# Where the second pair's sums of weight blocks are made in a fused attention and gated-MLP kernel

## The chip, the cores and the metric

The kernel runs on one core of a Trainium2 chip. A core has five engines that run side by side, each through its own instruction stream in order: TensorE (PE, the matmuls, whose weight loads are shown apart as PEld), VectorE (DVE), ScalarE (ACT), GpSimd (POOL) and SyncE (SP, which here only issues DMAs). DMAs are issued from the streams of SP and ACT: a DMA whose buffer isn't free yet, or whose data isn't made yet, holds what stands behind it in the same stream. Sixteen DMA engines carry all transfers. Matmul results land in PSUM, which has eight banks here of 128 x 512 fp32.

The metric is the time of one execution on the device in microseconds (us); lower is better. The kernel before takes 739.52 us, the median of three runs from 738.2 to 742.48.

## The reference

Two branches read the same layer-normed input `xn` (2048 rows, 512 columns, fp32), and their product is added to `x`.

```
xn = layernorm(x)
# branch A: 32 heads of 16; each row attends to 8 rows: itself and those 2, 4, .. 14 back
q, k, v = split(xn @ wqkv)
s = windowed_attention(q, k, v) @ wo

# branch B: gMLP with F = 1792, Fh = 896
z  = gelu(xn @ w_in)                       # first projection: z1, second: the gate's
z1 = z[:, :896];  z2 = layernorm(z[:, 896:])
g  = w_sp @ z2 + b_sp                      # the mixing over the 2048 rows
b  = (z1 * g) @ w_out

out = x + s * silu(b)
```

## The kernel before

**Precision.** Every fp32 operand of a large matmul is split into a high part (rounded by ScalarE, `AF.Copy` to fp32r, L191) and a low part (the rest, by VectorE, L192). A product is three matmuls: high by high, high by low, low by high. `prep` (L171) fetches a raw 128 x 512 weight block by an SP DMA (`fetch`, L166), and splits it into one of eight weight pairs.

**Order of the stages on TensorE.** First q, k and v (`pair`, L379 to L381, stored to DRAM), then z1 (L649: seven blocks `f` of 128 columns, four row chunks `c` each, gelu, stored to DRAM by ACT as `z_d`), then the gate's second projection, called z2 (L735: an index `i` over eight pairs of row tiles `i` and `8 + i`), then the mixing (matmuls at L771), then `b` (L1000 to L1002) and last `s`, which needs attention's output.

**Attention** runs beside all this on VectorE, with GpSimd for one fold: `scores` (L523), `heads` (L530), `weighted` (L567), and a transpose (L590) whose result SP stores as `o_d` (L593). It is traced with the lowest priority (except `heads`), so it fills VectorE where nothing else is ready.

**The mixing.** The transposed `w_sp` is a grid of four column chunks `c` of 512 output rows and 16 blocks of 128 input rows. A pair `a` is the two chunks 2a and 2a + 1. With the input rows halved (blocks 0 to 7 and 8 to 15), each pair is a 2 x 2 block matrix, which is multiplied with z2 (halved by rows, and by columns into three blocks on either side of an odd one) in seven block products instead of eight. Each product is called m1 to m7 with the pair's letter, and runs over eight blocks `s` (`block_product`, L794); with the odd column it has 12 matmuls for each block. m1 and m2 use weight blocks as they are in the input. The products m3 to m7 use sums of weight blocks, and z2 operands that are combined in the z2 stage (`combine`, L709, stored as `t_d`). Order: m1a, m1b, m2a, m2b, m6a, m6b, m7 twice, m4 twice, m5a, m5b, m3a, m3b.

**The sums.** For each pair and each `i` of 8, `block_sums` (L635) loads the four blocks of that index into two tiles of 128 x 1024, makes four sums in place on VectorE (L645), and stores the two tiles to `sums_d` in DRAM (ACT's queue, L646 and L647), from where m3 to m7 fetch them as weights. In the kernel before, sets 0 to 6 of pair 0 are traced in the z1 loop, one behind each `f`. Set 7 of pair 0 and all eight of pair 1 are steps between the block groups of m1a and m1b.

**Buffers that matter here.** `raws`: four tiles of 128 x 512 (256 KB each), the landing place of every raw weight of z1, z2 and the mixing. `t4`: eight tiles of 128 x 1024, used for z1's results, z2's results, the sums, the combined operands fetched again, the evictions between products (`kept`, tiles `xa` and `xb`, L930, and the tile `oo`) and the stored z1 tiles that the gates read (`stored_gates`, L848, which then seeds the banks again at L789 for m6a and m6b). A tile's next user waits until its last reader is through, a store included.

**What sets the order.** A planner puts each engine's instructions into a fixed order when the kernel is built: by program order as priority, as far as its cost model holds an instruction and its buffer for ready. At run time the order within an engine doesn't change. The raw block `(0, 0)` of m1a is split ahead into a weight pair of its own (`early_pair`, L726); `spatial_block(0, 1)` is traced in the last `i` of z2, the other raw blocks in the products.

Of the kernel before, what the change touches and what calls it, by code (L numbers as in the profile page):

```python
# [24 lines left out]
FB = FH // P  # L25
NG = 3
CT = 512
NC = S // CT
JC = NT // NC
HT = NT // 2  # L30
# [27 lines left out]
def kernel(  # L58
# [13 lines left out]
    nc = tc.nc  # L72
    pins = [True]

    def pin(ins):
        return tc.keep_in_program_order(ins) if pins[0] else ins
# [22 lines left out]
    sums_d = dram.tile([2, 2, HT, P, 2, CT], F32, name="sums_d")  # L99
# [54 lines left out]
    def mm(name):  # L154
        return ps.tile([P, 512], F32, tag=f"bank{next(turn)}", name=name)
# [10 lines left out]
    def fetch(src, n, name):  # L166
        raw = raws.tile([P, 512], F32, tag="raw", name=name + "r", bufs=RAW)
        pin(nc.sync.dma_start(raw[:, :n], src))
        return raw

    def prep(src, n, name, raw=None):  # L171
        if raw is None:
            raw = fetch(src, n, name)
        hi, lo = weight_pair(name)
        split(hi[:, :n], lo[:, :n], raw[:, :n])
        return hi, lo
# [299 lines left out]
    def t4(name, n=2):  # L476
        t = wide.tile([P, 2 * CT], F32, tag="t4", name=name, bufs=WIDE)
        return t.rearrange("p (i t) -> p i t", i=2)[:, :n]
# [153 lines left out]

    attention()

    def block_sums(a, i):  # L635
        top, low = t4(f"sa_{a}_{i}"), t4(f"sb_{a}_{i}")
        nc.sync.dma_start(top, w_sp[2 * a : 2 * a + 2, i].rearrange("c p t -> p c t"))
        nc.sync.dma_start(low, w_sp[2 * a : 2 * a + 2, HT + i].rearrange("c p t -> p c t"))
        for out_, p_, q_ in (
            (low[:, 1], top[:, 1], low[:, 1]),  # L640
            (top[:, 1], top[:, 0], top[:, 1]),
            (top[:, 0], top[:, 0], low[:, 1]),
            (low[:, 0], top[:, 0], low[:, 0]),
        ):
            nc.vector.tensor_tensor(out_, p_, q_, op=ALU.add)  # L645
        nc.scalar.dma_start(sums_d[a, 0, i], top)  # L646
        nc.scalar.dma_start(sums_d[a, 1, i], low)  # L647

    for f in range(FB):  # L649
        wh, wl = prep(w_in1[:, f, :], KB * P, f"w1_{f}")  # L650
        for c in range(NC):
            pz = mm(f"z1_{f}_{c}")
            for k in range(KB):
                cc = slice(k * P, (k + 1) * P)
                xh, xl = [planes[:, FB - KB + k, c * JC : (c + 1) * JC, a] for a in range(2)]
                nc.tensor.matmul(pz, wh[:, cc], xh, start=k == 0, stop=False)  # L656
                nc.tensor.matmul(pz, wh[:, cc], xl, start=False, stop=False)  # L657
                nc.tensor.matmul(pz, wl[:, cc], xh, start=False, stop=k == KB - 1)  # L658
            if c % 2 == 0:
                zp = t4(f"z1t_{f}_{c}")  # L660
            zt = zp[:, c % 2]
            if c == 0:
                nc.vector.tensor_tensor(zt, pz, rb, op=ALU.mult)
                pz = zt
            nc.scalar.activation(zt, pz, AF.Gelu_apprx_tanh)  # L665
            if c % 2:
                nc.scalar.dma_start(z1_d[f, c - 1 : c + 1].rearrange("c p t -> p c t"), zp)
        block_sums(0, f)

    HALF = (slice(0, 512), slice(512, FH))  # L670
    WID = (512, FH - 512)
# [6 lines left out]
    def z2_half(j, h, zt):  # L678
        xh, xl = xn_at(j)
        pz = mm(f"z2_{j}_{h}")[:, : WID[h]]  # L680
        for k in range(KB):
            wh, wl = [w[:, : WID[h]] for w in w2[k, h]]
            nc.tensor.matmul(pz, xh[:, k], wh, start=k == 0, stop=False)  # L683
            nc.tensor.matmul(pz, xh[:, k], wl, start=False, stop=False)  # L684
            nc.tensor.matmul(pz, xl[:, k], wh, start=False, stop=k == KB - 1)  # L685
        nc.scalar.activation(zt[:, HALF[h]], pz, AF.Gelu_apprx_tanh, scale=late_rstd(j))

    def spatial_block(c, js):
        return prep(w_sp[c, js], CT, f"wsp_{c}_{js}")

    def z2_stats(j, zt):
        st = const.tile([P, 2, 6], F32, tag="st2", name=f"zst_{j}", bufs=3)
        mv, nm = mvz[:, j], nmz[:, j : j + 1]
        for h in range(2):
            nc.vector.bn_stats(st[:, h], zt[:, h * FQ : (h + 1) * FQ])
        nc.vector.bn_aggr(mv, st)
        nc.gpsimd.tensor_tensor(nm, mv[:, 0:1], mone, op=ALU.mult)
        nc.gpsimd.tensor_scalar(mv[:, 1:2], mv[:, 1:2], EPS, None, op0=ALU.add)
        nc.gpsimd.tensor_tensor(mv[:, 1:2], mv[:, 1:2], nhalf, op=ALU.pow)
        nc.gpsimd.tensor_tensor(nm, nm, mv[:, 1:2], op=ALU.mult)  # L700

    def z2_normal(j, zt, n):
        zh, zl = z2_at(j)
        nc.scalar.activation(zt, zt, AF.Identity, bias=nmz[:, j : j + 1], scale=mvz[:, j, 1:2])  # L704
        split(zh[:, :n], zl[:, :n], blocks(zt, FB)[:, :n])
# [3 lines left out]
    def combine(i, zts):  # L709
        b11, b12, b21, b22 = [z[:, p_] for z in zts for p_ in (first_part, last_part)]  # L710
        for out_, p_, q_, op in (
            (b11, b11, b12, ALU.subtract),
            (b12, b12, b22, ALU.subtract),
            (b22, b22, b11, ALU.add),
            (b21, b21, b22, ALU.subtract),
        ):
            nc.vector.tensor_tensor(out_, p_, q_, op=op)
        split(*[t[:, ODD + 1 :] for t in z2_at(i)], blocks(b22, ODD))
        v = b11
        src = bass.AP(  # L720
            tensor=v.tensor, offset=v.offset, ap=[list(v.ap[0]), [FH - F3, 2], [1, F3]]
        )
        nc.scalar.dma_start(t_d[:2, i].rearrange("a p t -> p a t"), src)
        nc.scalar.dma_start(t_d[2, i], b21)
# [9 lines left out]
    raw_z = {}  # L734
    for i in range(HT + 2):  # L735
        if i < HT:
            raw_z[i] = [t4(f"zt_{j}").rearrange("p i t -> p (i t)")[:, :FH] for j in (i, HT + i)]
            for h in range(2):
                for j, zt in zip((i, HT + i), raw_z[i]):
                    z2_half(j, h, zt)  # L740
                if i == HT - 1 and h == 0:
                    spatial[0, 1] = spatial_block(0, 1)
        if 0 < i <= HT:
            for j, zt in zip((i - 1, HT + i - 1), raw_z[i - 1]):
                z2_stats(j, zt)
        if i > 1:
            for j, zt, n in zip((i - 2, HT + i - 2), raw_z[i - 2], (ODD + 1, FB)):
                z2_normal(j, zt, n)
            combine(i - 2, raw_z[i - 2])
# [25 lines left out]
    def z2_block(j, f):  # L775
        return [planes[:, f, j, a] for a in range(2)]
# [7 lines left out]
    for n in range(8):  # L784
        a, f = n // 2 % 2, n // 4 * 2 + n % 2
# [8 lines left out]
    def block_product(a, name, z, w, odd=None, start=False, stop=False, steps=()):  # L794
        for n, s0 in enumerate(range(0, HT, 2)):
            pair_ = [(s, w(s)) for s in (s0, s0 + 1)]
            for f in range(ODD):
                for s, wp in pair_:
                    three(banks[a, f], z(s, f), wp, start and s == 0, s == HT - 1, not start)
            if odd:  # L800
                for s, wp in pair_:
                    three(banks[a, ODD], odd(s), wp, False, s == HT - 1, True)
            for do in steps[n] if steps else ():
                do()

    def plain(a, c, r):
        def w(s):
            js = r * HT + s
            return spatial.get((2 * a + c, js)) or spatial_block(2 * a + c, js)

        return w
# [15 lines left out]
    def at(r, f0):  # L827
        return lambda s, f: z2_block(r * HT + s, f0 + f)

    def odd(r):  # L830
        return lambda s: z2_block(r * HT + s, ODD)
# [9 lines left out]
    def later(fn, *args):  # L841
        return lambda: fn(*args)
# [57 lines left out]

    T1, T3, T4 = [[later(operand, i, s0) for s0 in range(0, HT, 2)] for i in range(3)]

    def sums(a, i):
        return later(block_sums, a, i)


    with urgent(300):
        for f in range(ODD + 1):
# [2 lines left out]
    def second_seeds():  # L911
# [10 lines left out]

    block_product(
        0, "m1a", at(0, 0), plain(0, 0, 0), odd(0),
        steps=([second_seeds, sums(0, 7)], [sums(1, 0)], [sums(1, 1)], [sums(1, 2)]),
    )
    oo = t4("oo")
    os2 = [oo[:, 0], oo[:, 1]]

    def kept(a):  # L930
# [6 lines left out]
        nc.vector.tensor_tensor(biases[a][1], biases[a][0], biases[a][1], op=ALU.add)  # L937

    kept(0)
    block_product(  # L940
        1, "m1b", at(0, 0), plain(1, 0, 0), odd(0),
        steps=([sums(1, 3)], [sums(1, 4)], [sums(1, 5), sums(1, 6)], [sums(1, 7)]),
    )
    kept(1)
    block_product(
        0, "m2a", at(1, 0), plain(0, 0, 1), odd(1),
        steps=([T3[0]], [T3[1]], [T3[2]], [T3[3]]),
# [13 lines left out]
    for a in range(2):  # L961
        block_product(
            a, "m7", at(0, 0), summed(a, 0, 1), odd(0),
            steps=([T1[2 * a]], [], [T1[2 * a + 1]], []),
# [3 lines left out]
    for a in range(2):  # L968
# [5 lines left out]
        steps=([], [], [], [later(late, 0, ODD, 1)]),  # L974
# [5 lines left out]
        steps=([], [], [], [later(late, 1, ODD, 1)]),  # L980
# [25 lines left out]
    for i, j in enumerate(rows_of):  # L1006
        c, jj = divmod(j, JC)
# [98 lines left out]
```

## Time and profile before

| | before |
|---|---|
| median of three runs | 739.52 us |
| profiled execution | 738.82 us |
| span of its instructions | 737.0 us |
| PE busy | 694.2 us (94%) |
| DVE busy | 611.9 us (83%) |
| ACT busy | 284.5 us (39%) |
| POOL busy | 115.2 us (16%) |
| DMA traffic | 182.37 MB, mean 247 GB/s |

"Busy" counts the engine's own instructions, not DMA issues or waits. The span is the time from the first instruction to the last; some 1.8 us of the profiled execution lie outside it. In an answer of the trace, `[10.48 <-DMA sums_d<-sa]` behind an instruction says that its engine sat idle for 10.48 us before it, and that what came last was the DMA that stores the tile `sa` to `sums_d`. `zt`, `sa`, `sb`, `xa`, `zl`, `tr` and `bt` are names of t4 tiles; names like `wsp_9r` are raw tiles, with `h` and `l` the split pair; `BIG` holds the split activations, `g` are the mixing's PSUM banks. The index in `wsp_9` is the block among the 16.

### The profile page before, as it was taken

The numbers are of one execution on the slowest core, as the hardware profiler recorded it, in microseconds if no ns is written. First come the engines' busy times: TensorE is split into PE (matmuls) and PEld (weight loads), VectorE is DVE, ScalarE is ACT, GpSimd is POOL, SyncE is SP. The second block draws the span as 40 slices with busy tenths as digits, with TensorE's granted clock in tenths as the row PEclk, the third lists the DMA queues.
The fourth block names the chain that finished last, engine by engine and source line by source line (L and its number), as shares of the span: only waits on it lengthen the run. The fifth ranks groups of instructions, "written<-read, shape, count | busy, mean of one in ns | idle before, by whom it ended". The sixth has DMA issues, their size and how long they took to land.

```text
span 737.0 us, 9252 instructions
## 1 busy us (share of the span) xinstructions
PE 694.2 (94%) x3084; PEld 576.9 (78%) x3084; DVE 611.9 (83%) x902; ACT 284.5 (39%) x458; POOL 115.2 (16%) x110
## 2 busy tenths in 40 slices
PE   8999999999999999996956389999999999999998
PEld 7888888888889999784845268888888888888886
DVE  6763679998999899999999999899999999510374
ACT  4343332352333576753211335343343444221521
POOL 2100002221114555311112111111111100000000
PEclk9999999999999999998987789999999999999999
DMA  8776787799899142689999997668646685451695
GB/s 277 233 209 209 205 267 211 207 324 345 290 387 364 58 154 72 201 269 388 371 382 379 334 322 274 233 231 286 222 153 224 202 273 186 158 205 68 235 300 192
DMA packets 109952, 182.37 MB, mean 247 GB/s; under 512 B 10064, under 2 KB 50256, under 8 KB 109904
## 3 DMA queue, kind: packets, MB, share of 16 engines
q1 hardware_dynamic: 69152, 130.79, 53.5%
q10 hardware_dynamic: 40752, 50.99, 19.3%
q8 instruction: 24, 0.39, 0.2%
q14 instruction: 24, 0.20, 0.1%
HBM read 122.42 MB, written 59.32 MB: 247 GB/s over the span
## 4 chain that ended last, share of the span: by engine, by line
PE 69%; DVE 14%; DMA 8%; issue 4%; ACT 3%; POOL 2%; SPq 1%; ACTq 0%; DVEq 0%
PE g L771 26%; PE qkv L380 5%; PE qkv L381 5%; PE qkv L379 5%; PE b L1002 3%; PE b L1001 3%; PE b L1000 3%; PE z L658 3%; PE z L657 3%; PE z L656 3%; PE s L1002 2%; PE s L1001 2%; PE s L1000 2%; DMA o_d<-tt 2%; DVE pr L523 2%
## 5 line engine op out<-in xcount | busy, mean ns | idle before, releaser
L577 POOL TENSOR_TENSOR pv<-pv 128x1024 f32<-128x1024 f32 x29 | 69.5, 2398 | 397.2 <-DVE pv L567 397.1
L523 DVE TENSOR_TENSOR pr<-k,q 128x2048 f32<-128x2048 f32 x32 | 73.2, 2287 | 6.2 <-DMA q<-qkv_d 4.4
L567 DVE TENSOR_TENSOR pv<-v,lg 128x2048 f32<-128x2048 f32 x32 | 73.1, 2286 | 0.4
L530 DVE TENSOR_REDUCE lg<-pr 128x128 f32<-128x2048 f32 x32 | 72.9, 2277 | 0.0
L396 ACT ACTIVATE stage<-qkv 128x512 f32<-128x512 f32 x36 | 21.4, 595 | 49.3 <-PE qkv L381 49.3
L771 PE MATMUL g<-ws_0h,BIG 128*128 128x512 f32 x52 | 19.9, 401 | 15.4 <-ACT g L789 15.4
L771 PE MATMUL g<-wsp_8h,BIG 128*128 128x512 f32 x32 | 13.7, 429 | 17.7 <-ACT xa L792 17.7
L192 DVE TENSOR_TENSOR o_1l<-ol,o_1h 128x512 fp32r<-128x512 f32 x3 | 2.1, 688 | 32.8 <-ACT o_1h L191 32.8
L1011 ACT ACTIVATE bt<-b 128x512 f32<-128x512 f32 x16 | 9.4, 594 | 44.0 <-PE b L1002 44.0
L704 ACT ACTIVATE zt<-zt,nmz,mvz 128x896 f32<-128x896 f32 x16 | 18.0, 1133 | 21.0 <-POOL nmz L700 19.2
L645 DVE TENSOR_TENSOR sb<-sa,sb 128x512 f32<-128x512 f32 x32 | 22.9, 727 | 3.0 <-DMA sb<-in_w_sp 2.5
L1055 DVE TENSOR_TENSOR sg<-s,sg 128x512 f32<-128x512 f32 (+1 forms) x17 | 11.2, 659 | 16.9 <-PE s L1002 16.1
L685 PE MATMUL z<-w_0h,BIG 128*128 128x512 f32 x64 | 25.0, 391 | 0.0
L684 PE MATMUL z<-w_0l,BIG 128*128 128x512 f32 x64 | 25.0, 391 | 0.0
L683 PE MATMUL z<-w_0h,BIG 128*128 128x512 f32 x64 | 24.9, 389 | 0.0
L771 PEld LDWEIGHTS g<-ws_0h,BIG 128*128 128x128 f32 x52 | 10.0, 192 | 17.9 <-ACT g L789 15.8
L771 PEld LDWEIGHTS g<-wsp_8h,BIG 128*128 128x128 f32 x32 | 6.5, 203 | 20.2 <-ACT xa L792 18.9
L275 DVE TENSOR_TENSOR xT<-xT,mr 128x512 f32<-128x512 f32 x20 | 13.8, 688 | 9.8 <-DMA mr<-mv_d 6.2
L582 DVE TENSOR_TENSOR pv<-pv 128x512 f32<-128x512 f32 x32 | 21.8, 680 | 0.0
L665 ACT ACTIVATE z1t<-z 128x512 f32<-128x512 f32 x21 | 12.5, 594 | 23.3 <-PE z L658 17.3
L685 PE MATMUL z<-w_1h,BIG 128*128 128x384 f32 x64 | 21.3, 336 | 0.0
L683 PE MATMUL z<-w_1h,BIG 128*128 128x384 f32 x64 | 21.3, 335 | 0.0
(461 smaller groups left out, 2256.1 us busy)
## 6 DMA issues: line engine op xcount, KB each, us to landing
qkv_d<-stage ACTq DMA_DIRECT2D x24, 512.0 KB
k<-qkv_d SPq DMA_DIRECT2D x16, 704.0 KB
v<-qkv_d SPq DMA_DIRECT2D x16, 704.0 KB
sa<-in_w_sp SPq DMA_DIRECT2D x16, 512.0 KB
sb<-in_w_sp SPq DMA_DIRECT2D x16, 512.0 KB
sums_d<-sa ACTq DMA_DIRECT2D x16, 512.0 KB
sums_d<-sb ACTq DMA_DIRECT2D x16, 512.0 KB
z_d<-z1t ACTq DMA_DIRECT2D x14, 512.0 KB
```

Of the source, the lines that this page charges most:

```text
L379: nc.tensor.matmul(pq, xh[:, k], wh, start=k == 0, stop=False)
L380: nc.tensor.matmul(pq, xh[:, k], wl, start=False, stop=False)
L381: nc.tensor.matmul(pq, xl[:, k], wh, start=False, stop=k == KB - 1)
L523: line(nc.vector.tensor_tensor(pr, taps(ks[u], j0), qb.unsqueeze(1).to_broadcast([P, W, NJ * CS]), op=ALU.mult))
L530: line(nc.vector.tensor_reduce(lgs[u][:, :, j0 * HS : (j0 + NJ) * HS], pr.rearrange("p w (i d) -> p w i d", d=DH), axis=AX.X, op=ALU.add,))
L567: line(nc.vector.tensor_tensor(pv.rearrange("p w (i d) -> p w i d", d=DH), taps(vs[u], j0).rearrange("p w (i d) -> p w i d", d=DH), lgs[u] ...
L577: eng.tensor_tensor(pv[:, 0:4], pv[:, 0:4], pv[:, 4:8], op=ALU.add)
L683: nc.tensor.matmul(pz, xh[:, k], wh, start=k == 0, stop=False)
L685: nc.tensor.matmul(pz, xl[:, k], wh, start=False, stop=k == KB - 1)
L771: nc.tensor.matmul(pg, z[a], w[b], start=start and i == 0, stop=stop and i == 2, skip_group_check=seeded)
L1000: nc.tensor.matmul(pp[:, cols], hi, wh, start=k == 0, stop=False)
L1001: nc.tensor.matmul(pp[:, cols], hi, wl, start=False, stop=False)
```

## The change

Set 7 of pair 0 is made in the z1 loop too, behind set 0. The eight sets of pair 1 are made in the z2 loop, one at the head of each `i`. They don't use t4 tiles there but the four raw tiles: four loads of one block each through `fetch`, the same four sums in place, and four stores of one block each. The steps of m1a and m1b hold no sums any more. What is computed and what lies in `sums_d` stay the same.

```diff
-    def block_sums(a, i):
+    def pair_tiles(a, i):
         top, low = t4(f"sa_{a}_{i}"), t4(f"sb_{a}_{i}")
         nc.sync.dma_start(top, w_sp[2 * a : 2 * a + 2, i].rearrange("c p t -> p c t"))
         nc.sync.dma_start(low, w_sp[2 * a : 2 * a + 2, HT + i].rearrange("c p t -> p c t"))
-        for out_, p_, q_ in (
-            (low[:, 1], top[:, 1], low[:, 1]),
-            (top[:, 1], top[:, 0], top[:, 1]),
-            (top[:, 0], top[:, 0], low[:, 1]),
-            (low[:, 0], top[:, 0], low[:, 0]),
-        ):
+        return top, low, [top[:, 0], top[:, 1], low[:, 0], low[:, 1]]
+
+    def raw_tiles(a, i):
+        return [
+            fetch(w_sp[2 * a + c, r + i], CT, f"sr_{a}_{i}_{c}_{r}") for r in (0, HT) for c in range(2)
+        ]
+
+    def block_sums(a, i, whole_pairs=True):
+        if whole_pairs:
+            top, low, ts = pair_tiles(a, i)
+        else:
+            ts = raw_tiles(a, i)
+        t0, t1, l0, l1 = ts
+        for out_, p_, q_ in ((l1, t1, l1), (t1, t0, t1), (t0, t0, l1), (l0, t0, l0)):
             nc.vector.tensor_tensor(out_, p_, q_, op=ALU.add)
-        nc.scalar.dma_start(sums_d[a, 0, i], top)
-        nc.scalar.dma_start(sums_d[a, 1, i], low)
+        if whole_pairs:
+            nc.scalar.dma_start(sums_d[a, 0, i], top)
+            nc.scalar.dma_start(sums_d[a, 1, i], low)
+        else:
+            for n, t in enumerate(ts):
+                nc.scalar.dma_start(sums_d[a, n // 2, i, :, n % 2], t)
...
         block_sums(0, f)
+        if f == 0:
+            block_sums(0, FB)
...
         if i < HT:
+            block_sums(1, i, False)
             raw_z[i] = [t4(f"zt_{j}").rearrange("p i t -> p (i t)")[:, :FH] for j in (i, HT + i)]
...
-    def sums(a, i):
-        return later(block_sums, a, i)
...
     block_product(
         0, "m1a", at(0, 0), plain(0, 0, 0), odd(0),
-        steps=([second_seeds, sums(0, 7)], [sums(1, 0)], [sums(1, 1)], [sums(1, 2)]),
+        steps=([second_seeds], [], [], []),
     )
...
-    block_product(
-        1, "m1b", at(0, 0), plain(1, 0, 0), odd(0),
-        steps=([sums(1, 3)], [sums(1, 4)], [sums(1, 5), sums(1, 6)], [sums(1, 7)]),
-    )
+    block_product(1, "m1b", at(0, 0), plain(1, 0, 0), odd(0))
```

## The prediction

> **What bounds the kernel now.** I read the stretches by engine first, then TensorE's own waits, then the chain, then the timelines of the queues around the holes. Of each stretch the answer gives the start and end, its length, busy time and instructions of PE, PEld, DVE, ACT and POOL, the granted clock, the DMA share and GB/s.
>
> ```profile
> 250.00:300.00 50.00, 48.84 (x243) 43.57 (x242) 47.45 (x84) 36.26 (x56) 24.45 (x41) 1.00 0.28 92
> 300.00:350.00 50.00, 42.71 (x183) 34.51 (x183) 48.79 (x81) 25.15 (x41) 11.04 (x14) 0.95 0.90 310
> 350.00:400.00 50.00, 36.54 (x141) 28.45 (x141) 49.93 (x66) 8.12 (x16) 7.11 (x3) 0.85 1.01 377
> 400.00:450.00 50.00, 34.60 (x146) 28.13 (x145) 48.73 (x69) 21.23 (x36) 7.17 (x3) 0.83 0.96 335
> 500.00:550.00 50.00, 50.00 (x223) 41.39 (x222) 49.75 (x74) 16.85 (x29) 7.22 (x3) 1.00 0.68 228
> ```
>
> ```profile
> PE   8999999999999999996956389999999999999998
> ```
>
> By the slices of the page, TensorE is full except between 296 and 427 us, in the first four products of the mixing (m1a, m1b, m2a, m2b); there the DMA engines are full, while just before, in the gate's second projection, they stand at 0.28. VectorE is full in all five rows. TensorE's waits in 290 to 430 us (total, times, longest), and the last piece of the chain:
>
> ```profile
> PE g L771 <- ACT xa L792: 17.7, 2, 10.6
> PE g L771 <- ACT g L789: 15.4, 1, 15.4
> PE g L771 <- ACT wsp_12h L191: 2.4, 1, 2.4
> PE g L917 <- ACT zt L686: 1.2, 1, 1.2
> ```
> ```profile
> 426.52 187.05 PE g L771 x816
> ```
>
> The holes sum to 36.7 us. From 426.52 on TensorE runs without a break: 187.05/816 = 0.229 us for a matmul. So what the change is worth is where that 426.52, the start of m6a, goes. ScalarE's timeline shows who held the evictions:
>
> ```profile
> 376.39 0.63 ACT L191 ACTIVATE wsp_12h<-wsp_12r 128x512 fp32r<-128x512 f32 x1 [12.84 <-DMA sums_d<-sa]
> 392.35 1.09 ACT L792 ACTIVATE xa<-g 128x512 f32<-128x512 f32 x2 [10.48 <-DMA sums_d<-sa]
> ```
>
> Both idle times end with stores of the second pair's sums: the tiles that the evictions want (t4, eight buffers) are the tiles that the sums are made in. That is the hole the change aims at.
>
> **The change part by part.**
>
> *Removed from m1a and m1b:* nine sets of sums (one of pair 0, eight of pair 1), each four loads' worth of 256 KB in two DMAs, four adds, two stores. With them go the two waits on xa, the one on wsp_12h, and I take the 15.4 us on g (stored_gates waiting for z1 and x tiles, which also come out of t4) as gone too; its bounds are 0 and 15.4, and I take 0 since eight t4 buffers stand nearly empty without the sums. Then m1 and m2 cost their matmuls: 4 products x 8 blocks x 12 = 384; 12 (block 0, whose weights are split ahead in the early pair) can be done earlier; 372 x 0.229 = 85.3 us. Late next is whatever sets the start of m1.
>
> *Moved to the first block of z1:* one set. Its adds are 4 x 0.68 us on a VectorE whose slack is attention's; its two loads on SP and two stores on ACT stand ahead of z1's own:
>
> ```profile
> L590 DVE STREAM_TRANSPOSE tt<-pv x32: 383/434/449, 116.4 to 635.9; 128x256 f32<-128x256 f32 x32
> L1002 PE MATMUL s<-BIG x16: 389/389/389, 690.0 to 700.2; 128*128 128x512 f32 x16
> 226.11 0.60 ACT L686 ACTIVATE zt<-z 128x512 f32<-128x512 f32 x1 [1.77 <-DMA sums_d<-sb]
> ```
>
> Attention's last transpose is at 636 and its first use, the output product, at 690: VectorE has some 50 us to give before anything is late. The third row is the cost if cover is gone: z2's first evictions already wait 1.77 us for a t4 tile; one more set makes this longer, and eight PSUM banks of 12 matmuls (8 x 12 x 0.229 = 22 us) lie between that and TensorE. I take 0, bounds 0 and 2 us; a gain has no place here, TensorE being full in z1.
>
> *Moved to z2:* eight sets of pair 1, now in four raw tiles: 32 loads on SP, 32 adds, 32 stores on ACT (16 and 16 DMAs before). VectorE: 32 x 0.68 = 22 us, taken from attention; covered by the same 50 us. On SP a load that waits for its raw tile holds what is queued behind it, attention's loads and its o_d stores, which is covered by the 50 us too. On ACT a store that waits for its add holds z2's evictions; I cost that at 0 behind the PSUM banks, and its end is a rival below. What isn't covered is the raw ring. It has four buffers, one set fills it, and every raw weight of m1 from block 1 on is traced behind the eight sets, so is fetched behind them. Before, the ring stood so (SP's timeline, then the matmul that m1 began with):
>
> ```profile
> 211.47 0.35 SPq L168 DMA_DIRECT2D wsp_1r<-in_w_sp  x1
> 212.64 0.35 SPq L168 DMA_DIRECT2D wsp_2r<-in_w_sp  x1
> 213.85 0.33 SPq L168 DMA_DIRECT2D wsp_3r<-in_w_sp  x1
> 226.82 0.38 SPq L168 DMA_DIRECT2D wsp_4r<-in_w_sp  x1
> 295.75 0.35 SPq L168 DMA_DIRECT2D wsp_5r<-in_w_sp  x1
> 299.50 0.50 PE L917 MATMUL g<-wsp_0h,BIG 128*128 128x512 f32 x1 [1.16 <-ACT zt L686]
> ```
>
> The four buffers were free at 211.5 to 226.8 and then lay filled with m1's blocks 1 to 4 until z2 ended. In the changed kernel those four slots go to the first set, so its first add comes at 226.8 + 4.0 (landing) + 1.1 (pick-up) = 232. Then seven more rounds follow one another: a set's first add needs its fourth tile, which needs the last store of the set before to have landed. The rows for one round:
>
> ```profile
> 230.57 0.67 DVE L645 TENSOR_TENSOR sb<-sa,sb 128x512 f32<-128x512 f32 x1
> 232.67 0.63 DVE L645 TENSOR_TENSOR sa<-sa 128x512 f32<-128x512 f32 x1
> 234.09 0.62 DVE L645 TENSOR_TENSOR sa<-sa,sb 128x512 f32<-128x512 f32 x1
> 235.56 0.68 DVE L645 TENSOR_TENSOR sb<-sa,sb 128x512 f32<-128x512 f32 x1
> 238.59 0.33 ACTq L647 DMA_DIRECT2D sums_d<-sb  x1
> ```
> ```profile
> 236.66 3.28 DMA sums_d<-sa
> 327.84 2.49 DMA wsp_9r<-in_w_sp
> 340.93 6.09 DMA wsp_15r<-in_w_sp
> ```
>
> Adds, first start to last end: 5.7 us (four times 0.65 and other VectorE work between). To the store's issue: 2.35 in this set (236.24 to 238.59), nothing at the least; I take 0.8. Store landing: 3.28 for 512 KB, so 3.0 for 256 KB. SP's issue 0.35 and what stands ahead of it: 0.6. Load landing: 2.49 to 6.09, I take 4.0, nearer the low end as these loads come when the DMA engines are at about half. VectorE's pick-up: half of one attention operation, 1.1.
>
> ```profile
> L523 DVE TENSOR_TENSOR pr<-k,q 128x2048 f32<-128x2048 f32 x32 | 73.2, 2287 | 6.2 <-DMA q<-qkv_d 4.4
> ```
>
> Round: 5.7 + 0.8 + 3.0 + 0.6 + 4.0 + 1.1 = **15.2 us**. The Trainium skill, page DMA: Bandwidth & Descriptors, section Anatomy of one DMA, gives a transfer a fixed 2.0 us and bytes over 436 GB/s (for the GpSimd path); an estimate by that page is 2.6 us for 256 KB, and the sum with it would be a round of 13.4 and 732 us. The trace agrees with it in its shortest row (2.49) and not in its longest (6.09).
>
> Bounds of a round. Low: adds in 3.0 us, as the last set has them (first and last add below), and both landings at 2.5, the other terms kept: 10.5.
>
> ```profile
> 398.38 0.67 DVE L645 TENSOR_TENSOR sb<-sa,sb 128x512 f32<-128x512 f32 x1
> 400.70 0.68 DVE L645 TENSOR_TENSOR sb<-sa,sb 128x512 f32<-128x512 f32 x1
> ```
>
> High: a whole cycle of a set as the trace has it, load issue to last store, in z1 with full DMA engines:
>
> ```profile
> 150.75 0.44 SPq L637 DMA_DIRECT2D sa<-in_w_sp  x1
> 166.90 0.34 ACTq L647 DMA_DIRECT2D sums_d<-sb  x1
> ```
>
> 16.15 + 3.28 = 19.4 us; there two or three sets were in flight, here there is room for one.
>
> Sum: first add of the eighth set at 232 + 7 x 15.2 = 338.4. Its first slot is back when its third add has read it and its store has landed, 4.5 us on; then SP 0.6, landing 4.0, split on ScalarE 0.6: m1's block 1 at 348. Plus 85.3, plus 1.6 because TensorE comes back slow from an idle time. Behind the hole that ended at 348.29 it took 3.15 us for seven matmuls, 0.45 each instead of 0.229; the granted clock of 0.85 in that stretch has the same cause:
>
> ```profile
> 348.29 0.79 PE L771 MATMUL g<-wsp_8h,BIG 128*128 128x512 f32 x1 [7.12 <-ACT xa L792]
> 351.44 0.57 PE L771 MATMUL g<-wsp_10l,BIG 128*128 128x512 f32 x1
> ```
>
> So m6a starts at 435.1 instead of 426.52, **8.6 us later**. The four holes are gone and one of 48 us, from z2's end to 348, stands in their place. The profiled execution took 738.82 (span 737.0 and 1.82 around it); 738.82 + 8.6 = 747.4; the median of the runs is 0.7 above it, so 748. The formula for the rest: m6a at 328.7 + 7 x round; 14.0 us is where nothing changes.
>
> **The rivals.** Half a per cent, 3.7 us, is about what a measurement of this kernel tells from no change.
>
> *Landings at their shortest.* With 2.5 us for both transfers the round is 13.2, the first add 1.5 us and the tail 2 us earlier: m6a at 328.7 - 3.5 + 7 x 13.2 = 417.6, 8.9 us earlier, **731**. For it: DMA share 0.28 in z2, to which 64 transfers of 256 KB, 16.8 MB over some 100 us, add under a half. Against: attention's loads, 704 KB each, stand on the same queue. The Trainium skill's page named above gives about this time.
>
> *The ring keeps up.* Adds in 4.3 us as well, halfway between 3.0 and 5.7: round 11.8, m6a at 407.8, **721**; the end of this road is m1 starting when z2 ends, 299.5 + 85.3 = 384.8, or 41.7 us won and 698, which needs rounds of 8.5 us, under the low bound. For it: each set is traced ahead of the z2 work beside it, so it has priority there, and the last set had its 3.0 us. Against: VectorE is full in z2, and its other work fills every pause between two adds that depend on each other.
>
> *No change:* rounds between 13.4 and 14.5, **740**.
>
> *ScalarE's queue becomes z2's bound.* Each store waits in order on ScalarE for an add, and the evictions of z2 stand behind it.
>
> ```profile
> ACT zt L704 <- POOL nmz L700: 19.2, 5, 6.2
> ```
>
> ScalarE has 13.7 of 50 us idle in z2, some 21 of 76, and already waits 19.2 us there for GpSimd; 32 stores held 2.35 us each are 75, so z2 ends up to 54 us late, m1 at 353.6, m6a at 440.5, **753**. It decides only from a mean hold of 2.2 us on, where z2's end passes the ring's 348.
>
> *The holes have another cause.* If the 15.4 us before m6a are the z1 loads on a queue that blocks, not t4, they come again: 748 + 15.4 = **763**.
>
> **How the numbers follow.** Forecast, rounds of 14.5 to 19.4 us: 0.36, its own range 743 to 777. Shortest landings 0.18, ring keeps up 0.20: faster 0.38. No change 0.12. ScalarE's queue 0.06 and the second cause 0.08: with the forecast, slower 0.50. For 8 in 10 the range goes from 716 (rounds of 11.1 us at the short landings, which leaves some 0.07 of the ring that keeps up) to 777 (rounds of 19.4).
>
> **What would show it.** Right: SP issues the first raw weight of m1 behind the sums at some 343 us, TensorE's one long idle time is there, and it no longer waits for xa; between first adds of successive sets lie 15 us; m2b follows m2a without a hole; attention still ends near 636. Wrong: sets follow each other in under 13.5 us, and the first weight is fetched before 328; or TensorE idles inside z2, with evictions behind stores; or the hole before m6a is still there.

## The result, and the profile after

The changed kernel takes 783.22 us (782.7 to 785.29 in four runs) against 740.03 us: 1.0587 times as long, 95% interval 1.055 to 1.0624. The direction was forecast; the size, 43 us instead of 8, was not, and it lies 6 us outside the range.

The stretches by engine of the kernel after (columns as in the prediction):

```profile
250.00:300.00 50.00, 47.00 (x230) 41.40 (x229) 47.73 (x89) 31.89 (x48) 25.32 (x38) 0.98 0.50 173
300.00:350.00 50.00, 5.12 (x11) 2.74 (x10) 46.44 (x75) 16.05 (x25) 15.13 (x19) 0.53 0.62 192
350.00:400.00 50.00, 14.90 (x53) 11.66 (x54) 43.96 (x52) 7.18 (x12) 7.45 (x4) 0.59 0.70 232
400.00:450.00 50.00, 50.00 (x222) 41.40 (x221) 48.63 (x62) 18.57 (x31) 9.23 (x4) 1.00 0.81 266
```

TensorE stands still from 305.7 to 385.1 us, after m1's first weight block; behind that it is full, where the kernel before had its holes. TensorE's waits in 290 to 600 us, SP's issue of the weight that it waited for, and the matmul at the end of the hole:

```profile
PE g L786 <- ACT wsp_1h L191: 79.4, 1, 79.4
PE g L929 <- ACT zt L700: 2.3, 2, 1.8
PE g L786 <- ACT g L804: 1.1, 1, 1.1
PE g L786 <- DVE lg L545: 0.3, 1, 0.3
```
```profile
371.48 1.13 SPq L168 DMA_DIRECT2D sr_8r<-in_w_sp  x2
380.97 0.33 SPq L168 DMA_DIRECT2D wsp_1r<-in_w_sp  x1
```
```profile
385.09 1.22 PE L786 MATMUL g<-wsp_1h,BIG 128*128 128x512 f32 x2 [79.40 <-ACT wsp_1h L191]
472.33 0.39 PE L786 MATMUL g<-ws_0h,BIG 128*128 128x512 f32 x1
```

The waits on xa, on wsp_12h and on g before m6a are gone; in their place is one wait for m1's second raw weight, which was issued behind the last loads (`sr`) of the eighth set. m6a starts at 472.33 instead of 426.52, 45.8 us later, and that is the whole loss: the span is 44.5 us longer.

VectorE's timeline: the first add of the first set, all four of the second, the first and last of the sixth, and the first of the eighth:

```profile
236.27 0.67 DVE L653 TENSOR_TENSOR sr_8r<-sr_0r,sr_8r 128x512 f32<-128x512 f32 x1
...
258.32 0.66 DVE L653 TENSOR_TENSOR sr_8r<-sr_0r,sr_8r 128x512 f32<-128x512 f32 x1
...
263.57 0.67 DVE L653 TENSOR_TENSOR sr_0r<-sr_0r,sr_0r 128x512 f32<-128x512 f32 x1
...
270.74 0.68 DVE L653 TENSOR_TENSOR sr_0r<-sr_0r,sr_8r 128x512 f32<-128x512 f32 x1
...
273.80 0.68 DVE L653 TENSOR_TENSOR sr_8r<-sr_0r,sr_8r 128x512 f32<-128x512 f32 x1
...
347.74 0.69 DVE L653 TENSOR_TENSOR sr_8r<-sr_0r,sr_8r 128x512 f32<-128x512 f32 x1 [2.57 <-issue]
...
353.35 0.67 DVE L653 TENSOR_TENSOR sr_8r<-sr_0r,sr_8r 128x512 f32<-128x512 f32 x1
...
375.57 0.69 DVE L653 TENSOR_TENSOR sr_8r<-sr_0r,sr_8r 128x512 f32<-128x512 f32 x1 [2.70 <-DMA sr_8r<-in_w_sp]
```

From the first set's first add to the eighth's there are 139.3 us for seven rounds, 19.9 each. The second set's adds take 16.2 us from start to end, with z2's other VectorE work and some of attention's between them; the sixth set's, when z2's work is over, 6.3. Between the second set's adds VectorE was idle for 2.3 us in all. Before a set's first add it was idle only at the sixth set (2.57 us), the seventh (1.07) and the eighth (2.70).

### The profile page after: what moved, and what is told of

Same layout as the page of the kernel before. It is cut to its first block, busy times and chain, and to the rows that moved or that the text cites. A ratio compares the mean times of both kernels' runs of the same rounds, so it can differ in the third digit from the quotient of the medians.

```text
span 781.5 us, 9331 instructions
## 1 busy us (share of the span) xinstructions
PE 692.1 (89%) x3084; PEld 574.8 (74%) x3084; DVE 616.8 (79%) x902; ACT 285.0 (36%) x458; POOL 116.3 (15%) x110
## 4 chain that ended last, share of the span: by engine, by line
PE 67%; DVE 13%; DMA 11%; issue 5%; POOL 2%; ACT 1%; SPq 1%; DVEq 0%; ACTq 0%
PE g L786 21%; PE qkv L379 5%; PE qkv L380 5%; PE qkv L381 5%; PE b L1009 3%; PE z L669 3%; PE z L668 3%; PE b L1010 3%; PE b L1011 3%; PE z L670 3%; DVE pr L523 2%; PE s L1011 2%; PE s L1009 2%; PE s L1010 2%; DVE pv L567 2%
## 5 line engine op out<-in xcount | busy, mean ns | idle before, releaser
L786 PE MATMUL g<-wsp_1h,BIG 128*128 128x512 f32 x16 | 7.6, 513 | 79.4 <-ACT wsp_1h L191 79.4
L786 PEld LDWEIGHTS g<-wsp_1h,BIG 128*128 128x128 f32 x16 | 4.0, 258 | 80.7 <-ACT wsp_1h L191 79.9
L553 ACT ACTIVATE lg<-lg 128x256 f32<-128x256 f32 x16 | 6.6, 413 | 53.3 <-DVE tt L590 26.5
L1064 DVE TENSOR_TENSOR sg<-s,sg 128x512 f32<-128x512 f32 (+1 forms) x17 | 11.2, 658 | 16.9 <-PE s L1011 16.9
L191 ACT ACTIVATE BIG<-zl 128x512 fp32r<-128x512 f32 x20 | 12.5, 627 | 26.3 <-DVE zl L851 26.3
L698 PE MATMUL z<-w_1l,BIG 128*128 128x384 f32 x64 | 21.4, 335 | 0.0
L192 DVE TENSOR_TENSOR BIG<-zt,BIG 128x512 fp32r<-128x512 f32 (+2 forms) x24 | 18.5, 770 | 3.1 <-ACT BIG L191 3.1
```

The costliest lines, as they stand in the source:

```text
L786: nc.tensor.matmul(pg, z[a], w[b], start=start and i == 0, stop=stop and i == 2, skip_group_check=seeded)
```

## The experiments

Theory A is the prediction's: the four raw tiles hold one set at a time, m1's raw weights queue behind the last set, and in m1 and m2 the sums in t4 tiles were what made the holes. What was open was the round.

**What sets the round: no adds.** The 32 adds of the z2 sets are left out; their loads and stores stay, so weight blocks are stored in the place of pair 1's sums.

```diff
-        for out_, p_, q_ in ((l1, t1, l1), (t1, t0, t1), (t0, t0, l1), (l0, t0, l0)):
+        for out_, p_, q_ in ((l1, t1, l1), (t1, t0, t1), (t0, t0, l1), (l0, t0, l0)) if whole_pairs else ():
```

> The changed kernel without the 32 adds of the eight sets in z2; their loads and stores stay, so what is stored as sums is the weight blocks themselves. Theory A (VectorE's order sets the length of a round: adds spread over 13 to 16 us and started some 8 us after the data are there): without adds a round is a store of 3.7, an issue of 0.6 and a load of 3, some 8 to 9 us with the queues; the eighth set is out by about 300 us, TensorE's hole of 79 us shrinks to under 15, and the time is 700 to 715 us. Rival B (the transfers and the two queues set the round): rounds stay at 15 us or more, m1's first raw weight comes after 340, time 748 us or more.

723.74 us, in one run: between the two. SP's issues (the second set's first loads, then m1's weight) and TensorE's wait:

```profile
234.75 5.27 SPq L168 DMA_DIRECT2D sr_0r<-in_w_sp  x2
...
316.85 0.33 SPq L168 DMA_DIRECT2D wsp_1r<-in_w_sp  x1
```
```profile
PE g L786 <- ACT wsp_1h L191: 17.1, 1, 17.1
```

Seven rounds in 82.1 us, 11.7 each, against 19.6 between the same points of the changed kernel (243.83 to 380.97). The adds are worth 8 us of a round. The 11.7 left is more than the 8 to 9 that I gave the transfers and queues, and less than rival B's 15; what fills it beside a load and a store wasn't split further.

**Is it VectorE: the adds on GpSimd.**

```diff
-            nc.vector.tensor_tensor(out_, p_, q_, op=ALU.add)
+            (nc.vector if whole_pairs else nc.gpsimd).tensor_tensor(out_, p_, q_, op=ALU.add)
```

> The changed kernel with the 32 adds of the z2 sets on GpSimd instead of VectorE. Without adds the first raw weight of m1 was issued at 316.9, with them on VectorE at 381.0, so the adds cost 8 us a round. Theory A1 (what costs is VectorE's full stream): GpSimd is idle half of z2, an add is about 1.2 us there, four take 5 to 6 us, so m1's first weight comes at 355 to 365 and the time is 755 to 770 us. Rival A2 (a chain of four adds is placed late whatever the engine): 778 us or more.

767.4 us, in one run, inside A1's band. GpSimd's first and last add of the second set, and m1's weight:

```profile
264.27 1.29 POOL L653 TENSOR_TENSOR sr_8r<-sr_0r,sr_8r 128x512 f32<-128x512 f32 x1
...
270.16 1.58 POOL L653 TENSOR_TENSOR sr_8r<-sr_0r,sr_8r 128x512 f32<-128x512 f32 x1
```
```profile
364.67 0.35 SPq L168 DMA_DIRECT2D wsp_1r<-in_w_sp  x1
```

An add is twice as long there, yet this set's four take 7.5 us instead of 16.2, and the first seven sets' 7.8 each instead of 10.8. So most of what four adds take on VectorE in z2 comes from what stands between them in its fixed order, not from the adds (4 x 0.67 = 2.7 us). A round is 16.9 us here (246.60 to 364.67, between the same points as above): 2.7 less than with the adds on VectorE, and still 5.2 more than without them. Why the planner places the adds so far apart on VectorE, no run here shows.

**Is it the raw ring: the sums of z2 in t4 tiles.**

```diff
-            block_sums(1, i, False)
+            block_sums(1, i)
```

> The eight sets stay in z2 but are made in t4 tiles (two loads, two stores a set) instead of the raw tiles. Theory A (the raw ring: m1's weights queue behind the eight sets): m1's raw weights are fetched before z2 ends as in the kernel before, the hole of 79 us is gone, and what remains are waits of z2's evictions for t4 tiles: 705 to 740 us. Rival C (VectorE and ScalarE are overloaded in z2 and m1 is late for its operands, whatever the tiles): TensorE still idles 40 us or more around the end of z2, time 755 us or more.

751.93 us, 1.0149 (1.0112 to 1.0185): between the bands. SP's issue of m1's second weight is back where it was, and no wait for it is left. TensorE's waits are others:

```profile
214.53 0.40 SPq L168 DMA_DIRECT2D wsp_1r<-in_w_sp  x1
```
```profile
PE z L697 <- ACT zt L700: 25.8, 6, 6.2
PE g L929 <- ACT zt L700: 12.7, 2, 11.8
```

The wait for wsp_1h is gone without the sums in the raw ring, as theory A says. But TensorE now waits 38.5 us for z2's evictions, more than the band allowed for and close to the 40 that rival C asks for. The amount of work alone doesn't explain them: in the changed kernel the same 32 adds stand in z2, and evictions hold TensorE for 2.3 us. The longest of ScalarE's own waits before these evictions (L700) end with users of t4 tiles: the adds in `sb` (9.2 us), the stores `t_d<-zt` (5.7), work on `zt` (4.8). That speaks for the tiles; I haven't split the 38.5 between them and ScalarE's order.

**How the hole goes with the number of sets: four and three.** The rest are steps of m1 again, in t4 tiles. The edit for four (for three the bound is 3, and set 3 is a step of m1a):

```diff
-            block_sums(1, i, False)
+            if i < 4:
+                block_sums(1, i, False)
...
+        steps=([sums(1, 4)], [sums(1, 5)], [sums(1, 6)], [sums(1, 7)]),
```

> Only sets 0 to 3 of pair 1 are made in z2 (raw tiles); sets 4 to 7 are steps of m1b in t4 tiles, as before. Theory A: m1's block 1 starts 9.5 us behind the first add of the last set in the ring; the fourth set's was at 305.9, so m1 goes on at about 315 instead of 385, and m1 to m2 get back at most 4/9 of their 36.7 us of holes: 783 - 70 + 0 to 16 = 713 to 729 us. Rival C: halving the work in z2 halves the delay: 745 to 760 us.

> Sets 0 to 2 of pair 1 in z2 (raw tiles), set 3 a step of m1a and 4 to 7 of m1b in t4 tiles. Theory A: the third set's first add was at 284.0, plus 9.5 is 293.5, before z2 ends: the hole of 14 + 4 us that four sets left is gone, and 734 - 18 = 716 us if five sets in t4 tiles hold m1 and m2 no more than four did; to 726 if they do in proportion. Rival C (z2 itself is stretched by the sums in it): 730 us or more.

Four sets: 734.06 us, 0.9916 (0.9887 to 0.9944), 5 us above the band. Three: 727.63 us, 0.9827 (0.9807 to 0.9848), 1.6 us above it. m1's second weight (SP) and TensorE's wait for it, with four sets, then the weight with three:

```profile
315.98 0.33 SPq L168 DMA_DIRECT2D wsp_1r<-in_w_sp  x1
```
```profile
PE g L787 <- ACT wsp_1h L191: 14.0, 1, 14.0
```
```profile
295.00 0.34 SPq L168 DMA_DIRECT2D wsp_1r<-in_w_sp  x1
```

With three sets no wait for it is left. Eight sets, 79 us; four, 14; three, none: the ring decides, and z2 covers three sets. Behind it, with three sets, m1 and m2 had other waits again, 8.3 us on g the largest.

**What the sums in m1 and m2 cost: none for pair 1.** Its products read pair 0's sums instead.

```diff
-            block_sums(1, i, False)
...
-        return lambda s: prep(sums_d[a, half_, s, :, i], CT, f"ws_{a}{half_}{i}_{s}")
+        return lambda s: prep(sums_d[0, half_, s, :, i], CT, f"ws_{a}{half_}{i}_{s}")
```

> No sums of pair 1 at all; its products read pair 0's stored sums instead. This prices the first half of the change by itself. Theory A (the four holes of m1 and m2 come from the sums in t4 tiles): m1 starts at z2's end near 299 us, m6a at 385 to 390, time 698 to 705 us. Rival D (the hole before m6a has another cause): 15 us or so of it stays, time 712 us or more.

697.02 us, in one run; m6a starts at

```profile
386.29 0.39 PE L785 MATMUL g<-ws_0h,BIG 128*128 128x512 f32 x1
```

and no hole before it is over 1.6 us. All four holes, the 15.4 us on g among them, came with making the sums in m1 and m2 (set 7 of pair 0 is in z1 here, as in the changed kernel). This run takes away their tiles, their adds and their traffic together, so it doesn't tell these apart.

**The set moved to z1, alone,** in the kernel before:

```diff
         block_sums(0, f)
+        if f == 0:
+            block_sums(0, FB)
...
-        steps=([second_seeds, sums(0, 7)], [sums(1, 0)], [sums(1, 1)], [sums(1, 2)]),
+        steps=([second_seeds], [sums(1, 0)], [sums(1, 1)], [sums(1, 2)]),
```

> The kernel before with one part of the change alone: set 7 of pair 0 made in the z1 loop. Theory: its place in z1 costs nothing (0 to 2 us were the bounds), and m1 has eight sets instead of nine, so at most 36.7/9 = 4 us come back: 735 to 740 us. Rival: the t4 tiles it takes in z1 push z2 and all behind it: 742 us or more.

743.83 us, 1.005 (1.0031 to 1.0069): slower by half a per cent, against my 0, and on the rival's side (742 or more). The waits of TensorE in m1 and m2 hardly change, and m6a is 2.9 us later:

```profile
PE g L773 <- ACT xa L794: 19.8, 2, 11.2
PE g L773 <- ACT g L791: 12.9, 1, 12.9
PE g L773 <- ACT wsp_1h L191: 2.0, 1, 2.0
```
```profile
429.44 0.79 PE L773 MATMUL g<-ws_0h,BIG 128*128 128x512 f32 x1 [12.85 <-ACT g L791]
```

**A version that beats both: three sets in z2, the others spread.** m1a has no sums, m1b has sets 3 to 6, m2b set 7.

```diff
+            if i < 3:
+                block_sums(1, i, False)
...
+        steps=([sums(1, 3)], [sums(1, 4)], [sums(1, 5)], [sums(1, 6)]),
...
-    block_product(1, "m2b", at(1, 0), plain(1, 0, 1), odd(1))
+    block_product(1, "m2b", at(1, 0), plain(1, 0, 1), odd(1), steps=([sums(1, 7)], [], [], []))
```

> As with three sets, but the other five are spread: sets 3 to 6 in m1b, one a step, and set 7 in m2b. Theory: m1a has no sums at all, so its evictions find t4 tiles free: 712 to 720 us. Rival: the place of the five doesn't matter: the same as with three sets within 3 us.

723.93 us, 0.9774 (0.9756 to 0.9793), the fastest here that makes all the sums. It lies 4 us above the theory's band and 3.7 us below the run with three sets, so the place of the five matters, but less than I thought.

**Its parts.** Only spread, nothing moved to z2 or z1 (sets 0 to 3 in m1b, 4 to 7 in m2b); three sets in z2 without the set in z1 (that one goes to m1b, sets 6 and 7 to m2b); two sets in z2 instead of three (sets 2 to 5 in m1b, 6 and 7 in m2b). The edits, cut; the first is against the kernel before, the second against the kernel after, the third against three sets, spread:

```diff
# spread only
+        steps=([second_seeds, sums(0, 7)], [], [], []),
...
+        steps=([sums(1, 0)], [sums(1, 1)], [sums(1, 2)], [sums(1, 3)]),
...
+    block_product(1, "m2b", at(1, 0), plain(1, 0, 1), odd(1), steps=([sums(1, 4)], [sums(1, 5)], [sums(1, 6)], [sums(1, 7)]))
# three sets without the set in z1
-        if f == 0:
-            block_sums(0, FB)
...
+        steps=([sums(0, 7)], [sums(1, 3)], [sums(1, 4)], [sums(1, 5)]),
...
# two sets
-            if i < 3:
+            if i < 2:
...
```

> The kernel before with nothing moved to z2 or z1: set 7 of pair 0 stays in m1a, sets 0 to 3 of pair 1 are steps of m1b and 4 to 7 of m2b. It asks whether three sets in z2 help, or only that m1a is free of sums. Theory A (both help, since the DMA engines are idle in z2 and full in m1 and m2): faster than before, but short of 724: 726 to 736 us. Rival E (only the place in m1 and m2 matters): 720 to 726 us. Rival F (later sets collide with the loads of m6): 740 us or more.

> Three sets in z2, as in the run with three sets spread, but set 7 of pair 0 is taken out of the z1 loop: m1b holds it and sets 3 to 5, m2b sets 6 and 7. The set in z1 alone cost 3.7 us over the kernel before. Theory: it costs as much here: 720 to 722 us. Rival: one more set in m1b costs what z1 gives: 724 us or more.

> Two sets in z2, sets 2 to 5 in m1b, 6 and 7 in m2b; set 7 of pair 0 in z1. Theory A: with three sets the ring was free when z2 ended, so a smaller number gives nothing there and one more set loads m2: 724 to 728 us. Rival: three sets already hold m1's first weights back by some us: 718 to 722 us.

| | time, us | ratio (interval) | m6a starts | from there to the end of the span |
|---|---|---|---|---|
| before | 740.03 | | 426.52 | 310.5 |
| spread only | 739.09 | 0.9993 (0.9973 to 1.0012) | 399.99 | 337.1 |
| three without the set in z1 | 734.12 | 0.9911 (0.9883 to 0.9938) | 397.00 | 335.7 |
| two sets | 726.71 | 0.982 (0.9793 to 0.9846) | 399.23 | 324.5 |
| three sets, spread | 723.93 | 0.9774 (0.9756 to 0.9793) | 398.19 | 321.8 |
| no second pair's sums | 697.02 | one run | 386.29 | 308.9 |

Each ratio is against runs of the kernel before that were made beside that kernel. Two sets came out in the theory's band. Spread only did not: it lies 3 us above its band and can't be told from the kernel before. Without the set in z1 the time is 12 us above what the theory gave, so there the rival's side (724 us or more) holds.

All four spread kernels start m6a within 3 us of each other and differ behind it. "Spread only", with four sets in m2b, shows it in two rows: the same hole before m6a, and another before m6b:

```profile
399.99 0.80 PE L771 MATMUL g<-ws_0h,BIG 128*128 128x512 f32 x1 [15.60 <-ACT g L789]
...
435.14 0.80 PE L771 MATMUL g<-ws_0h,BIG 128*128 128x512 f32 x1 [16.63 <-ACT g L789]
```

Spreading alone moves the holes; with three sets in z2 and one in z1, what is left behind m6a is 11 us more than before instead of 27. One thing stays open. The kernel without the set in z1 and the kernel with two sets have six sets each in the same places of m1b and m2b, and yet the one with a set in z1 is 7 us faster than the one with that set's worth in z2; all of it lies behind m6a, where the profiled executions differ by 11 us. The set in z1 cost 3.7 us alone and goes with a gain here, and no run says why the sign turns.

## Why the prediction was right and wrong

- *m1's weights queue behind the eight sets in the raw ring.* Right, and it is the whole of the slowdown: 79.4 us of wait for wsp_1h in place of the 36.7 us of holes, gone when the sums use other tiles.
- *The holes of m1 and m2 go, the 15.4 us too.* Right: from m1's restart to m6a I had 85.3 + 1.6 = 86.9 us, and 87.2 were measured (472.33 - 385.09). 697 us without any second pair's sums is the 698 that the prediction gave as the end of that road.
- *The round of 15.2 us* is the step that failed, and in it the term "adds, first start to last end: 5.7". Over the first seven sets the adds took 75.7 us, 10.8 each: 13.0 to 16.2 in the four sets that meet z2's work and its tail, 6.3 to 6.5 in the others. The rest of a round, 19.9 - 10.8 = 9.1, is on average what the prediction had for it (9.5), but not round by round, so that agreement is partly luck. The first two sets' first adds came 12 to 13 us behind the issue of their last load (223.60 to 236.27, 246.20 to 258.32), with VectorE busy all that time, and the seventh's 2.6 (357.83 to 360.42); I had 4.0 + 1.1 for landing and pick-up. Nor do the terms follow one another strictly: the third set's first loads were issued at 270.94, before the second set's last add at 273.80. That fits with the 8 us a round, and not 10.8, that leaving the adds out saved. I took 5.7 from the one set that stood at z2's beginning, and named VectorE's being full in z2 only as an argument against a still shorter figure. Four dependent adds in a full engine's fixed order cost what stands between them.

```profile
223.60 0.33 SPq L168 DMA_DIRECT2D sr_8r<-in_w_sp  x1
244.89 1.31 SPq L168 DMA_DIRECT2D sr_8r<-in_w_sp  x2
270.94 0.84 SPq L168 DMA_DIRECT2D sr_0r<-in_w_sp  x2
```
```profile
360.42 0.69 DVE L653 TENSOR_TENSOR sr_8r<-sr_0r,sr_8r 128x512 f32<-128x512 f32 x1 [1.07 <-DMA sr_8r<-in_w_sp]
```

- *First add at 232:* 236.3. With seven rounds 33 us longer and this 4 us later, 348 became 385.1; the tail behind the eighth set's first add was 9.5 us, forecast 9.7.
- *The set in z1 at 0, bounds 0 and 2:* wrong by itself (3.7, interval 2.3 to 5.1), and small beside the rest.
- *Attention covers VectorE's and SP's extra work:* right. Its last transpose came at 594 instead of near 636, likely because VectorE had TensorE's hole to work in: in the run without pair 1's sums, which has no such hole, it came at 633.
- *The upper bound of a round, 19.4 from a whole cycle in z1,* was not a bound: 19.9 on average, and 25.7 from the second set's first add to the third's (258.32 to 284.02). The range's upper end, with m6a at 464.5, hung on it; 472.33 is that plus 7 x 0.5 and the 4.3 us of the first add. The rule of the Trainium skill, page DMA: Bandwidth & Descriptors, section Anatomy of one DMA, would have made the round shorter still. Loads of 256 KB on the chain of the kernel after took 2.56 and 3.19 us, near the 2.6 worked out from it; stores of 256 KB took 3.70, 3.72 and once 5.92, longer. A store and the load behind it took 6.3 and 9.1 us against the 7.0 of the sum, so the transfers weren't the main thing that was wrong.

```profile
354.05 3.72 DMA sums_d<-sr_8r
357.83 2.56 DMA sr_8r<-in_w_sp
...
365.49 5.92 DMA sums_d<-sr_0r
...
372.26 3.19 DMA sr_8r<-in_w_sp
...
380.97 3.70 DMA sums_d<-sr_0r
```

- *ScalarE's queue as z2's bound:* didn't decide. TensorE waited 2.3 us for evictions.

## What to carry to other kernels

Before work is moved into an idle stage, ask which buffers it will hold there and who is next in line for them: a ring that held the next stage's prefetched weights for 70 us was idle only in the traffic figures. Price a load, compute, store loop in a ring of one set as a serial chain, and take the compute term from the stage where it will run, with that engine's other work between its steps. Move as many rounds as the stage covers (three here: 0.983, and 0.977 with the other sets spread) and not all (eight: 1.059).

## What the runs showed of the hardware that I had not expected

GpSimd took 1.3 us and more for an add of 128 x 512 fp32 that took VectorE 0.67. That was expected, but not that the four of a set would take 7.8 us on average instead of 5 to 6; they were still shorter there than on VectorE, whose order in z2 is fuller (47.7 of 50 us busy in the kernel after, against GpSimd's 25.3). It wasn't free: TensorE's wait for z2's evictions, 2.3 us in the changed kernel, was

```profile
PE g L929 <- ACT zt L700: 15.5, 2, 9.8
```

there. On GpSimd the short sequences that z2's normalisation waits for then stood among the adds. That this is the reason is likely, but it wasn't tried.
